# Probabilities as matmul weights for the retrieval heads of a sparse-attention and MoE kernel

## The chip, the cores and the metric

The kernel runs on one core of a Trainium2 chip. The metric is the device time of one execution in microseconds (us). The profile's span, from the first instruction to the last, is 1.7 us shorter than that time. Each group of kernels below was run on one chip together with runs of the kernel before. Undisturbed runs count as fast.

TensorE multiplies, VectorE (DVE) and ScalarE (ACT) do elementwise work, GpSimd (POOL) and SyncE (SP) issue DMAs. TensorE's results land in buffers of PSUM ("banks"; the tiles pA, pO and pV), and TensorE waits when the one that it needs has not been read out yet: 0.4 us for ScalarE's relu (hs) and 1.1 us for VectorE's accumulator (acc) in the profile before. "Evacuation" means this reading out.

## The reference

Eight attention heads over 4 batches of 768 positions, head width 64. Heads 0, 2 and 6 ("retrieval") see all earlier positions, the other five ("streaming") see 4 sink positions and a window of 64. Four experts follow, each two matrix products with a relu between, mixed by normalised domain probabilities.

```python
scores = scale * np.matmul(q, k.transpose(0, 1, 3, 2))
mask = np.where(retr, causal, causal & (is_sink | in_win))
a = np.exp(scores - max);  a = a / (a.sum(-1) + 1e-9)
x = np.matmul(a, v)                      # -> (3072, 512), heads side by side
p = domain_probs / (domain_probs.sum(-1) + 1e-9)
out = sum(p[:, e] * (np.maximum(x @ w1[e], 0) @ w2[e]) for e in range(4))
```

## The kernel before

The work goes in eight chunks of 384 positions, two for each batch. The MoE of chunk g runs on TensorE while the attention of chunk g+1 is mixed into it in small steps. The first chunk's attention stands alone, ahead of everything. The chunks of batch 0 transpose q and k on TensorE, the later ones by DMA. The value product of a head takes 128 columns of weights: 64 of values and 64 of ones, so that rows 64 to 127 of the result hold the sum of the probabilities, and the quotient is built as exp(-ln(sum)) on ScalarE and multiplied on VectorE, straight into xT, which the MoE reads with x's columns on partitions.

```python
def values(h):
    hp, u = divmod(h, 2)
    ps = pV.tile([P, 512], FP32, name="pV", bufs=2)
    # ... work: the head's pieces of probabilities
    for n, (es, t, o, q0, nq) in enumerate(work):
        nc.tensor.matmul(out=ps[:, q0 : q0 + nq], lhsT=v_tile(b, c, h)[:, t, :],
                         rhs=es[:, o : o + nq], start=(n == 0), stop=(n == len(work) - 1), ...)
    # ...
    nc.scalar.activation(out=rc[r, :], in_=ps[o, 0:CH], func=AF.Ln, bias=eps[o, :])
    def scale(r=r, ps=ps):
        nc.vector.tensor_tensor(out=xT[g][r, hp, :], in0=ps[r, 0:CH], in1=rc[r, :], op=ALU.mult)
    nc.scalar.activation(out=rc[r, :], in_=rc[r, :], func=AF.Exp, scale=-1.0)
    late.append(scale)          # issued after the next head's exponential
# ... later chunks:
    yield from scores(0)
    for h in range(1, H):
        if not by_dma and h % 2 == 0 and h // 2 + 1 < HP:
            yield from transposes(h // 2 + 1)      # two heads before they are read
        yield from both(scores(h), values(h - 1))
    yield from values(H - 1)
```

The softmax here doesn't subtract the row's maximum and nothing guards it: scores larger than these inputs give would overflow.

## Time and profile before

| | kernel before |
|---|---|
| time, first three runs | 413.33 us (413.29 to 413.35) |
| the two levels | 411.6 and 413.3 us; the profiled run took 411.59, the lower one |
| until the first MoE matmul | 22.87 us |
| first MoE chunk, with the second chunk's attention | 55.39 us |
| the rest | 331.64 us |

The three stretches are cut at the start of the first MoE matmul of chunk 0 and at that of chunk 1. This is the view of busy time in these three stretches; the columns are the stretch, its length, busy time with the number of instructions on TensorE, its weight loads, VectorE, ScalarE and GpSimd, then the granted TensorE clock (1.00 is full speed), the DMA share and GB/s. Lines of a timeline, further below and in the prediction, give the start and the length in us, the engine, the line of kernel.py, the operation, output<-input with shapes, and the count; in brackets how long the engine stood idle before and what released it.

```profile
0.00:22.87 22.87, 17.23 (x138) 12.49 (x139) 19.68 (x54) 13.46 (x28) 21.47 (x39) 1.00 1.25 163
22.87:78.26 55.39, 52.80 (x367) 29.64 (x365) 26.98 (x50) 34.86 (x77) 31.91 (x40) 1.00 1.49 183
78.26:409.90 331.64, 325.50 (x2169) 180.00 (x2167) 108.12 (x199) 192.56 (x404) 88.37 (x97) 1.00 0.72 81
```

In the last stretch TensorE has some 98% of the time; in the first, VectorE has 86% and TensorE less. The two need different reasoning. GpSimd's 21.47 us (94%) in the first stretch are for the most part the issuing of loads, about 13 us.

### The profile page before, as it was taken

The page shows a single profiled execution, that of the slowest core. Times are in us where ns is not written, and L with a number is a line of the kernel's source. Part 1 is how long each engine was busy: PE and PEld are TensorE (multiplying, and loading weights), DVE is VectorE, ACT ScalarE, POOL GpSimd, SP SyncE. Part 2 cuts the span into 40 slices and gives each one's busy share as a digit, 9 for nine tenths or more (in the row PEclk, how much of TensorE's full clock was granted, in tenths as well). Part 3 has the DMA queues.
Part 4 walks back from the last instruction along what each step waited for, and adds up shares of the span by engine and source line. Part 5 has one row for each costly group of instructions (what it writes and reads, how often), then busy time and mean ns, then how long its engine had stood idle before and what let it go on. Part 6 is the DMA issues. An engine that isn't in the chain of part 4 may idle for free.

```text
span 409.9 us, 6803 instructions
## 1 busy us (share of the span) xinstructions
PE 395.5 (97%) x2670; PEld 222.1 (54%) x2670; DVE 154.8 (38%) x302; ACT 240.9 (59%) x509; POOL 141.7 (35%) x176
## 2 busy tenths in 40 slices
PE   6789999999999999999999999999999999999995
PEld 4655555555555555555555555555555555545552
DVE  7975552224442234222423334224333233332222
ACT  2867874346775747566675548655665558653331
POOL 8946718459349268004920194000000000000000
PEclk9999999999999999999999999999999999999998
DMA  9999999999999999349964899149002000020002
GB/s 175 144 190 204 210 209 137 144 207 113 158 91 186 183 102 113 65 102 132 111 40 110 171 92 73 12 110 155 3 0 80 2 2 0 2 77 2 1 2 77
DMA packets 159988, 40.83 MB, mean 100 GB/s; under 512 B 150364, under 2 KB 154836, under 8 KB 159956
## 3 DMA queue, kind: packets, MB, share of 16 engines
q0 software_dynamic: 102592, 20.98, 61.0%
q1 hardware_dynamic: 54164, 18.62, 23.0%
q10 hardware_dynamic: 3200, 0.79, 1.0%
q8 instruction: 21, 0.34, 0.3%
q14 instruction: 11, 0.09, 0.1%
HBM read 43.57 MB, written 6.29 MB: 122 GB/s over the span
## 4 chain that ended last, share of the span: by engine, by line
PE 84%; ACT 9%; DVE 3%; issue 2%; DMA 1%; ACTq 0%; DVEq 0%
PE pO L749 38%; PE pA L728 36%; PE pA L561 4%; PE pV L609 4%; ACT rc L628 3%; ACT hs L741 2%; ACT rc L638 2%; ACT es L579 1%; DMA q<-in_q_dram 1%; DVE acc L765 1%; DVE vS L261 1%; DVE xT L633 1%; ACTq L328 0%; PE pO L355 0%; DVE kS L490 0%
## 5 line engine op out<-in xcount | busy, mean ns | idle before, releaser
L728 PE MATMUL pA<-xT,w1sb 128*128 128x384 f16 x1024 | 186.2, 326 | 2.1 <-DVE kS L490 0.9
L749 PE MATMUL pO<-w2sb,hs 128*128 128x512 f16 x768 | 180.5, 379 | 1.2 <-DVE acc L765 1.1
L741 ACT ACTIVATE hs<-pA 128x384 f16<-128x384 f32 x256 | 121.7, 493 | 86.3 <-PE pA L728 79.4
L728 PEld LDWEIGHTS <-w1sb 128*128 128x128 f16 x1024 | 96.5, 98 | 61.9 <-issue 2.7
L749 PEld LDWEIGHTS <-hs 128*128 128x128 f16 x768 | 72.9, 98 | 78.4 <-ACT hs L741 2.6
L765 DVE SCALAR_TENSOR_TENSOR acc<-pO,p_sb,acc 128x512 f32<-128x512 f32 x72 | 53.7, 750 | 86.8 <-PE pO L749 86.3
L579 ACT ACTIVATE es<-pA 128x512 f16<-128x512 f32 (+3 forms) x122 | 61.1, 512 | 21.0 <-PE pA L561 19.3
L628 ACT ACTIVATE rc<-pV,eps 64x384 f32<-64x384 f32 x60 | 34.5, 575 | 43.3 <-PE pV L609 42.3
L633 DVE TENSOR_TENSOR xT<-pV,rc 64x384 f16<-64x384 f32 x60 | 33.1, 552 | 26.2 <-ACT rc L638 22.5
L204 POOL DMA_DIRECT2D kSr<-in_k_dram x30 | 30.1, 1004 | 33.4 <-issue 13.1
L250 POOL DMA_DIRECT2D vS<-in_v_dram x30 | 30.4, 1025 | 26.1 <-PE pV L609 26.1
L200 POOL DMA_DIRECT2D kRr<-in_k_dram x18 | 14.1, 783 | 52.5 <-DMA kR<-kRr 48.5
L761 DVE TENSOR_SCALAR acc<-pO,p_sb 128x512 f32<-128x512 f32 x24 | 18.0, 750 | 37.4 <-PE pO L749 37.4
L638 ACT ACTIVATE rc<-rc 64x384 f32<-64x384 f32 x58 | 30.2, 521 | 1.8
L583 DVE TENSOR_TENSOR es<-es,mC 128x256 f16<-128x256 f16 (+1 forms) x42 | 10.8, 257 | 46.2 <-ACT es L579 45.9
L583 DVE TENSOR_TENSOR es<-es,mW 128x384 f16<-128x384 f16 x30 | 10.8, 359 | 44.6 <-ACT es L579 44.5
L561 PE MATMUL pA<-qT,kR 128*128 128x384 f16 (+2 forms) x120 | 25.0, 278 | 0.0
L609 PE MATMUL pV<-es,vR 128*128 128x384 f16 (+2 forms) x120 | 21.6, 278 | 0.0
L246 POOL DMA_DIRECT2D vR<-in_v_dram x24 | 19.2, 801 | 4.5 <-DMA w2sb<-in_moe_w_dram 4.4
L561 PEld LDWEIGHTS <-kS 128*128 128x128 f16 x255 | 13.7, 98 | 8.8 <-issue 2.0
L609 PEld LDWEIGHTS <-vS 128*128 128x128 f16 x255 | 13.4, 98 | 8.8 <-DVE vS L261 2.1
L561 PE MATMUL pA<-qT,kS 128*128 128x55 f16 (+4 forms) x255 | 16.4, 195 | 1.5 <-ACT es L579 1.4
(77 smaller groups left out, 159.0 us busy)
## 6 DMA issues: line engine op xcount, KB each, us to landing
out_dram<-acc SPq DMA_DIRECT2D x24, 256.0 KB
w1sb<-in_moe_w_dram POOLq DMA_DIRECT2D x4, 1024.0 KB, 15.2
w2sb<-in_moe_w_dram POOLq DMA_DIRECT2D x4, 1024.0 KB, 17.7
kSr<-in_k_dram POOLq DMA_DIRECT2D x30, 112.0 KB, 3.8
vS<-in_v_dram POOLq DMA_DIRECT2D x30, 112.0 KB, 4.4
q<-in_q_dram POOLq DMA_DIRECT2D x18, 128.0 KB, 4.3
vR<-in_v_dram POOLq DMA_DIRECT2D x24, 48.0 KB, 4.4
kRr<-in_k_dram POOLq DMA_DIRECT2D x18, 48.0 KB, 3.8
```

The lines of the kernel that those rows point to most:

```text
L204: gp.dma_start(out=kSr[:, :, SH.index(h), own(h)], in_=windows_of(k, b, h, c),)
L250: gp.dma_start(out=t[:, :, own(h)], in_=windows_of(v, b, h, c))
L561: nc.tensor.matmul(out=ps[:, o : o + nq], lhsT=key_tile(b, c, h, t), rhs=qTs[b, c][:, hp, q0 : q0 + nq], start=(n == 0 or not first), stop ...
L579: nc.scalar.activation(out=es[:, 0:cols], in_=ps[:, 0:cols], func=AF.Exp, scale=SC)
L609: nc.tensor.matmul(out=ps[:, q0 : q0 + nq], lhsT=v_tile(b, c, h)[:, t, :], rhs=es[:, o : o + nq], start=(n == 0), stop=(n == len(work) - 1 ...
L628: nc.scalar.activation(out=rc[r, :], in_=ps[o, 0:CH], func=AF.Ln, bias=eps[o, :])
L633: nc.vector.tensor_tensor(out=xT[g][r, hp, :], in0=ps[r, 0:CH], in1=rc[r, :], op=ALU.mult)
L638: nc.scalar.activation(out=rc[r, :], in_=rc[r, :], func=AF.Exp, scale=-1.0)
L728: nc.tensor.matmul(out=pss[ft][:, 0:CH], lhsT=w1sb[:, e * DMP + ct, ft * P : (ft + 1) * P], rhs=xT[g][:, ct, :], start=(ct == 0), stop=(ct ...
L741: nc.scalar.activation(out=hs[:, ft, :], in_=ps[:, 0:CH], func=AF.Relu)
L749: nc.tensor.matmul(out=ps_o, lhsT=hs[:, ft, j * P : (j + 1) * P], rhs=w2sb[:, e * FTP + ft, :], start=(ft == 0), stop=(ft == FTP - 1),)
L765: nc.vector.scalar_tensor_tensor(out=acc[nt], in0=ps_o, scalar=p_ap, in1=acc[nt], op0=ALU.mult, op1=ALU.add,)
```

## The change

Its intent: for retrieval heads, stop paying for 64 columns of ones. The probabilities become the weights, block by block, and 65 columns stream: 64 of values and one of ones. The result has queries on partitions, so the sum is one number for each partition, and the quotient needs no Ln and Exp. The price: x has to be transposed back, on TensorE in the first chunk and by DMA afterwards. To make pairs that fill a whole transpose, heads 2 and 6 share a column tile of xT, so head order changes to (h % 4, h // 4) in xT and in w1's rows. Heads of later chunks run in a new order, and the streaming heads' products are issued by a clock of matmul time, 1.3 us late.

```diff
-        vR.append(pers.tile([P, S // P, len(RH), P], FP16, name=f"vR{i}"))
+        vR.append(pers.tile([P, S // P, NR, D + 2], FP16, name=f"vR{i}"))
...
+        def values_r(h):
+            for n, (j, t, lhsT) in enumerate(work):      # 128x128 blocks of probabilities
+                nc.tensor.matmul(out=ps[:, j, 0 : D + 1], lhsT=lhsT,
+                                 rhs=vR[i][:, t, RH.index(h), 0 : D + 1], ...)
...
+            nc.vector.tensor_scalar(out=rs, in0=ps[:, :, D : D + 1], scalar1=1e-9, ..., op0=ALU.add)
+            nc.vector.reciprocal(out=rs, in_=rs)
+            nc.vector.tensor_tensor(out=x[:, :, half(u)], in0=ps[:, :, 0:D],
+                                    in1=rs.to_broadcast([P, 3, D]), op=ALU.mult)
+            if h != 2 and not first:
+                nc.sync.dma_start(out=xT[g][:, ct, :]..., in_=x..., transpose=True)
...
-            yield from scores(0)
-            for h in range(1, H):
-                if not by_dma and h % 2 == 0 and h // 2 + 1 < HP:
-                    yield from transposes(h // 2 + 1)
-                yield from both(scores(h), values(h - 1))
+            order = (0, 2, 6, 1, 3, 5, 7, 4) if by_dma else (0, 2, 1, 3, 6, 5, 7, 4)
+            for n, h in enumerate(order):
+                if not by_dma and n in (3, 5):
+                    yield from transposes(3 if n == 3 else 2)
+                yield from both(scores(h), iter(()) if last is None else values(last))
...
-                late.append(scale)
+                later(scale)                             # LAG = 1300.0 ns of matmul time
...
+                cts = (0, 1, 2, 3) if g == 0 else (2, 1, 3, 0)
```

Cut: the halves of w1's load, the fills of ones, the first chunk's calls of `x_transposes`.

More of the change, by code (lines that the diff above doesn't have):

```diff
@@ L62 @@
     RETR = (1, 0, 1, 0, 0, 0, 1, 0)
+    PLACE = [(h % HP, h // HP) for h in range(H)]
     RH = [h for h in range(H) if RETR[h]]
@@ L135, with half, own_v @@
     v_sinks = pers.tile([NS, 1, NSH * P], FP16, name="v_sinks")
+    x_pair = pers.tile([P, 3, P], FP16, name="x_pair")
+    x_one = pers.tile([P, 3, P], FP16, name="x_one")
+    def half(u):
+        return slice(u * D, (u + 1) * D)
     def own(h):
-        u = h % 2
-        return slice(u * D, (u + 1) * D)
+        return half(h % 2)
+    def own_v(h):
+        return half(PLACE[h][1])
     def key_tile(b, c, h, t):
@@ L246, in load_v @@
                 gp.dma_start(
-                    out=t[:, 3 * c : 3 * c + 3, own(h)], in_=rows_of(v, b, h, c)
+                    out=t[:, 3 * c : 3 * c + 3, 0:D], in_=rows_of(v, b, h, c)
                 )
@@ L250, in load_v @@
                 gp.dma_start(
-                    out=t[:, :, own(h)], in_=windows_of(v, b, h, c)
+                    out=t[:, :, own_v(h)], in_=windows_of(v, b, h, c)
                 )
@@ L254, in load_v @@
                 gp.dma_start(
-                    out=t[R0:P, TC * c : TC * (c + 1), own(h)],
+                    out=t[R0:P, TC * c : TC * (c + 1), own_v(h)],
                     in_=tiles_of(v, b, h, c),
@@ L259, in sink_row @@
     def sink_row(b, h, c):
-        t = v_tile(b, c, h)[:, :, own(h)]
+        t = v_tile(b, c, h)[:, :, own_v(h)]
         nc.vector.tensor_copy(
@@ L276, in load_w1 @@
     def load_w1(e, f0, f1):
-        gp.dma_start(
-            out=w1sb[:, e * DMP : (e + 1) * DMP, f0:f1],
-            in_=moe_w1[e].rearrange("(co ci) f -> ci co f", ci=P)[:, :, f0:f1],
-        )
+        x = moe_w1[e].rearrange("(u c d) f -> u d c f", u=2, c=DMP)
+        for u in range(2):
+            gp.dma_start(
+                out=w1sb[half(u), e * DMP : (e + 1) * DMP, f0:f1],
+                in_=x[u, :, :, f0:f1],
+            )
     def load_w2(e):
@@ L309, in one_values_r @@
         t = slice(3 * c, 3 * c + 3)
-        fill(eng, vR[i][:, t, :, D:P], ONES)
+        fill(eng, vR[i][:, t, :, D : D + 2], ONES)
     def one_values(eng, c):
@@ L316, in one_values @@
         fill(eng, vS[0:R0, t, :, :].rearrange("p t h x -> p t (h x)"), ONES)
-        fill(eng, vS[:, t, 0:2, 0:D], ONES)
-        fill(eng, vS[:, t, 2, D:P], ONES)
-        fill(eng, vS[:, t, 3:5, 0:D], ONES)
-    assert all(h % 2 == 0 for h in RH) and [h % 2 for h in SH] == [1, 1, 0, 1, 1]
+        fill(eng, vS[:, t, 0:2, D:P], ONES)
+        fill(eng, vS[:, t, 2:5, 0:D], ONES)
+    assert RH == [0, 2, 6] and [PLACE[h] for h in RH] == [(0, 0), (2, 0), (2, 1)]
+    assert [PLACE[h][1] for h in SH] == [0, 0, 1, 1, 1]
     q32 = moe.tile([P, 3, H, D], FP32, name="q32", tag="hs", bufs=2)
@@ L547, in attention @@
         scale_of = {}
-        late = []
-        def run_late():
-            while late:
-                late.pop(0)()
         def scores(h):
@@ L589, in scores @@
                 es_of[h].append((es, parts))
-                run_late()
+                if first:
+                    tick(LAG)
                 yield ns
+        def values_r(h):
+            ps = pV.tile([P, 512], FP32, name="pV", bufs=2)
+            if first:
+                warm_up(ps, {6: 8}.get(h, 0), 256)
+            ps = ps[:, 0 : 3 * (D + 2)].rearrange("p (j x) -> p j x", j=3)
+            work = []
+            for j in range(3):
+                for es, parts in es_of[h]:
+                    for t, o, q0, nq in parts:
+                        x = j * P - q0
+                        if 0 <= x < nq:
+                            work.append((j, t, es[:, o + x : o + x + P]))
+            ns = 0
+            for n, (j, t, lhsT) in enumerate(work):
+                nc.tensor.matmul(
+                    out=ps[:, j, 0 : D + 1],
+                    lhsT=lhsT,
+                    rhs=vR[i][:, t, RH.index(h), 0 : D + 1],
+                    start=(n == 0),
+                    stop=(n == len(work) - 1),
+                    skip_group_check=True,
+                )
+                ns += mm_ns(D + 1)
+                if ns > 200 and n < len(work) - 1:
+                    yield ns
+                    ns = 0
+            rs = att.tile([P, 3, 1], FP32, name="rs", bufs=2)
+            nc.vector.tensor_scalar(
+                out=rs, in0=ps[:, :, D : D + 1], scalar1=1e-9, scalar2=None,
+                op0=ALU.add,
+            )
+            nc.vector.reciprocal(out=rs, in_=rs)
+            ct, u = PLACE[h]
+            x = x_pair if ct else x_one
+            nc.vector.tensor_tensor(
+                out=x[:, :, half(u)], in0=ps[:, :, 0:D],
+                in1=rs.to_broadcast([P, 3, D]), op=ALU.mult,
+            )
+            yield ns
+            if h != 2 and not first:
+                nc.sync.dma_start(
+                    out=xT[g][:, ct, :].rearrange("p (j x) -> p j x", j=3),
+                    in_=x.rearrange("p j x -> p (j x)"),
+                    transpose=True,
+                )
@@ L593, in values, with x_transposes @@
+        def x_transposes(h):
+            ct = PLACE[h][0]
+            x = x_pair if ct else x_one
+            r = slice(0, P) if ct else half(0)
+            ps = pO.tile([P, 512], FP32, name="pO", bufs=2)
+            for j in range(3):
+                nc.tensor.matmul(
+                    out=ps[r, j * P : (j + 1) * P], lhsT=x[:, j, r], rhs=ident16,
+                    start=True, stop=True,
+                )
+            nc.vector.tensor_copy(out=xT[g][r, ct, :], in_=ps[r, 0:CH])
         def values(h):
-            hp, u = divmod(h, 2)
+            if RETR[h]:
+                yield from values_r(h)
+                return
+            ct, u = PLACE[h]
@@ L599, in values @@
             if first:
-                warm_up(ps, {3: 4, 4: 4, 5: 6, 6: 8, 7: 10}.get(h, 0), 256)
+                warm_up(ps, {3: 4, 4: 4, 5: 6, 7: 10}.get(h, 0), 256)
             work = []
@@ L604, in values @@
                     work.append((es, t, o, q0, nq))
-            if RETR[h]:
-                work.sort(key=lambda w: -w[4])
             ns = 0
@@ L620, in values @@
                     ns = 0
-            r = slice(u * D, (u + 1) * D)
-            o = slice((1 - u) * D, (2 - u) * D)
-            pair = first and hp < HP - 1
-            if u == 0 or not pair:
-                rc_of[hp] = att.tile([P, CH], FP32, name="rc", bufs=4)
-            rc = rc_of[hp]
+            r, o = half(u), half(1 - u)
+            pair = first and h in (3, 4)
+            if not pair or u == 0:
+                rc_of[0] = att.tile([P, CH], FP32, name="rc", bufs=4)
+            rc = rc_of[0]
             nc.scalar.activation(
@@ L633, in scale @@
                 nc.vector.tensor_tensor(
-                    out=xT[g][r, hp, :], in0=ps[r, 0:CH], in1=rc[r, :], op=ALU.mult
+                    out=xT[g][r, ct, :], in0=ps[r, 0:CH], in1=rc[r, :], op=ALU.mult
                 )
@@ L638, in values @@
                 nc.scalar.activation(out=rc[r, :], in_=rc[r, :], func=AF.Exp, scale=-1.0)
-                late.append(scale)
+                later(scale)
             elif u == 0:
-                scale_of[hp] = scale
+                scale_of[0] = scale
             else:
                 nc.scalar.activation(out=rc, in_=rc, func=AF.Exp, scale=-1.0)
-                late.extend([scale_of[hp], scale])
+                later(scale_of[0])
+                later(scale)
             yield ns
@@ L677, in attention @@
                 sinks(*{3: [4, 5], 5: [7]}.get(h, []))
+                if h == 3:
+                    x_transposes(0)
                 if h == 5:
@@ L681, in attention @@
             yield from values(H - 1)
+            x_transposes(H - 2)
         else:
             sink_rows(b, c)
-            yield from scores(0)
-            for h in range(1, H):
-                if not by_dma and h % 2 == 0 and h // 2 + 1 < HP:
-                    yield from transposes(h // 2 + 1)
-                yield from both(scores(h), values(h - 1))
-            yield from values(H - 1)
-        run_late()
+            order = (0, 2, 6, 1, 3, 5, 7, 4) if by_dma else (0, 2, 1, 3, 6, 5, 7, 4)
+            last = None
+            for n, h in enumerate(order):
+                if not by_dma and n in (3, 5):
+                    yield from transposes(3 if n == 3 else 2)
+                yield from both(scores(h), iter(()) if last is None else values(last))
+                last = h
+            yield from values(last)
     def small_things():
@@ L713, with later, tick @@
     sink_k = {}
+    behind = []
+    clock = [0.0]
+    LAG = 1300.0
+    def later(op):
+        behind.append((clock[0] + LAG, op))
+    def tick(ns):
+        clock[0] += ns
+        while behind and behind[0][0] <= clock[0]:
+            behind.pop(0)[1]()
     def moe_group(g):
@@ L725, in moe_group, with layer1 @@
                 pss = {ft: bank() for ft in range(f0, f0 + (1 if f0 else ahead))}
-                def layer1(ft, ct):
+                cts = (0, 1, 2, 3) if g == 0 else (2, 1, 3, 0)
+                def layer1(ft, n):
+                    ct = cts[n]
                     nc.tensor.matmul(
@@ L731, in layer1 @@
                         rhs=xT[g][:, ct, :],
-                        start=(ct == 0),
-                        stop=(ct == DMP - 1),
+                        start=(n == 0),
+                        stop=(n == DMP - 1),
                     )
@@ L771, in moe_group @@
                 yield FTP // 2 * mm_ns(DM)
+    nc.vector.memset(x_one[:, :, D:P], 0.0)
     warm_up(ps_warm, 8, 512)
-    for _ in attention(0, 0):
-        pass
+    for ns in attention(0, 0):
+        tick(ns)
+    tick(LAG)
     zero(gp, kRr)
@@ L798 @@
         end = {0: 2.2}.get(g, 0.90 * E) * UNIT
-        att_ns = 3700.0 if nxt % NCH == 0 else 6800.0
+        att_ns = 3500.0 if nxt % NCH == 0 else 5600.0
         if nxt < NCH:
@@ L807 @@
             spent += ns
+            tick(ns)
             if to_transpose and spent > 0.5 * E * UNIT:
@@ L815 @@
                 done += step
-        for _ in att_steps:
-            pass
+                tick(step)
+        for ns in att_steps:
+            tick(ns)
+        tick(LAG)
 _INS = ['q', 'k', 'v', 'is_retrieval', 'n_sink', 'window', 'moe_domain_probs', 'moe_w1', 'moe_w2']
```

## The prediction

> **What bounds the kernel now.** I read the page's busy table and clock row first, then its chain that ended last, then the groups by shape, and last the matmul stream itself in order of time.
>
> ```profile
> PE 395.5 (97%) x2670; PEld 222.1 (54%) x2670; DVE 154.8 (38%) x302; ACT 240.9 (59%) x509; POOL 141.7 (35%) x176
> PEclk9999999999999999999999999999999999999998
> PE 84%; ACT 9%; DVE 3%; issue 2%; DMA 1%; ACTq 0%; DVEq 0%
> ...
> L728 PE MATMUL pA<-xT,w1sb 128*128 128x384 f16 x1024 | 186.2, 326 | 2.1 <-DVE kS L490 0.9
> L749 PE MATMUL pO<-w2sb,hs 128*128 128x512 f16 x768 | 180.5, 379 | 1.2 <-DVE acc L765 1.1
> ...
> L628 ACT ACTIVATE rc<-pV,eps 64x384 f32<-64x384 f32 x60 | 34.5, 575 | 43.3 <-PE pV L609 42.3
> L633 DVE TENSOR_TENSOR xT<-pV,rc 64x384 f16<-64x384 f32 x60 | 33.1, 552 | 26.2 <-ACT rc L638 22.5
> ...
> L638 ACT ACTIVATE rc<-rc 64x384 f32<-64x384 f32 x58 | 30.2, 521 | 1.8
> ```
>
> The reader is to see three things: TensorE is busy 97% at full clock and holds 84% of the chain; the two MoE groups are most of it; and ScalarE and VectorE have room on average. But the "mean ns" of a matmul holds its latency; what a matmul costs a full stream is the distance from its start to the next start. Worked out from the trace's start times, the medians are 216 ns for 512 columns, 162 for 384, 109 for 256, 56 for 128, 42 for 96 and 28 for 54 to 64, all with a weight load in front of each. So the bill of the span of 409.9 us is: 22.9 us until the first MoE matmul; 1024 x 0.1625 + 768 x 0.216 = 332.3 us of MoE; about 43 us of attention matmuls of the later seven groups, mixed in; 4.0 us tail after the last matmul; and some 8 us left over, in which TensorE stands (about 3 before 60 us, 4.9 after). Any matmul nanosecond removed after 23 us comes off the time, one for one.
>
> **What the Trainium skill says.** "TensorE: Matmul & The Clock Gate", section Back-to-back issue gap, gives N/2.4 + 2.5 ns as the isolated gap and about 81 ns for 128 columns in a stream of weight load and matmul pairs. This trace agrees with the first (56 ns at 128, 42 at 96, 109 at 256, each with its own weights) and not with the second. The same page, LDWEIGHTS (loading the stationary operand), charges by weight columns, P/1.2 = 107 ns for 128; the rows here show 98 ns, yet pairs with 54 columns follow one another every 28 ns, so the loads overlap and don't set the pace above 28 ns. "ScalarE: Activation LUTs", section What ACT_TABLE_LOAD costs, gives 0.833 ns an element plus 186 ns, or 280 ns with a bias pointer: 506 and 600 ns for 384 elements; measured 521 and 575. "Perfetto Trace Analysis", section Optimizing Scalar/DVE Operations, puts VectorE's fixed cost from PSUM at about 125 ns; the 384-wide product took 552 = 400 (384 at 0.96 GHz) + 152, near that.
>
> **The change part by part.**
>
> Value matmuls of the three retrieval heads. Before, the values (padded to 128 columns by ones) were the weights and 128 to 384 probabilities streamed. The groups by shape count 48 of 384 columns, 36 of 256, 36 of 128: 48 x 0.1625 + 36 x 0.109 + 36 x 0.056 = 13.7 us (13.8 by the starts). A first-half chunk's head is seen whole here, 93.06 to 93.39 = 0.33 us for three matmuls, and a stream of short pairs beside it: seven in 0.36 us, of which 0.19 is the last one's latency, so 28 ns apart:
>
> ```profile
> 93.06 0.49 PE L609 MATMUL pV<-es,vR 128*128 128x384 f16 x3
> 93.39 1.46 PE L728 MATMUL pA<-xT,w1sb 128*128 128x384 f16 x8
> ...
> 137.44 0.36 PE L609 MATMUL pV<-es,vS 128*128 128x54 f16 x7
> ```
>
> After, each 128x128 block of probabilities is a weight and 65 columns stream. Blocks are columns / 128: 6 in a first-half chunk, 15 in a second-half chunk, so 21 x 3 heads x 4 batches = 252 matmuls. At 65/2.4 + 2.5 = 29.6 ns (between the 28 measured at 64 and 42 at 96) that is 7.5 us. Saved 6.3 us, of which 0.45 lies in the very first chunk, where TensorE isn't the bound: **-5.8 us** on the path.
>
> The quotient. Before, ScalarE did Ln (575) and Exp (521) per head and VectorE the product (552). After, retrieval heads use VectorE alone: an add on 3 elements, a reciprocal on 3 (a 24-element pair of these took 178 + 302 ns; I take 300 for both), and a 192-wide product, 200 + 152 = 350: 0.65 us. VectorE gains 24 x 0.1 = 2.4 us, unnoticed at 38%. ScalarE loses 24 x 1.1 = 26 us, idle time nobody waits for, except where its bursts stop TensorE. The matmul stream shows the same five stops in each pair of groups, three times over: 0.31 us at 139.6 and 0.15 at 187.7 (Ln and Exp sit before the relu or the exponential that must free a PSUM bank), 0.30 at 152.6, 0.21 at 156.6, and the longest here:
>
> ```profile
> 169.76 0.52 ACT L638 ACTIVATE rc<-rc 64x384 f32<-64x384 f32 x1
> 170.31 0.56 DVE L633 TENSOR_TENSOR xT<-pV,rc 64x384 f16<-64x384 f32 x1 [1.11 <-ACT rc L638]
> 170.91 1.41 DVE L765 SCALAR_TENSOR_TENSOR acc<-pO,p_sb,acc 128x512 f32<-128x512 f32 x2
> 171.68 0.99 SPq L770 DMA_DIRECT2D out_dram<-acc  x2
> 171.71 1.02 PE L749 MATMUL pO<-w2sb,hs 128*128 128x512 f16 x4 [0.37 <-DVE acc L765]
> ```
>
> Here VectorE, in order, waits 1.11 us for ScalarE's Exp while a finished accumulator waits behind it, and TensorE stops for the bank (0.53 us by the starts). Retrieval heads now come first, so no Ln and Exp mixes with the 512-wide exponentials, and the products of the other heads are issued 1.3 us of matmul time later. I expect four of the five stops to go and 0.30 to stay: **-3.5 us** of the 4.9.
>
> Transposes. Queries now lie on partitions, so two DMA transposes of 128x384 per later group carry x back to xT, on SyncE. The three transposes of q (128x512 each) take 4.1 to 4.9 us of the queue a group, so about 1.2 us each here. Pair and single are done by some 60% of the previous group at the latest, over 15 us before they are read: hidden, **0**.
>
> The first chunk. It transposes on TensorE (6 matmuls, 0.3 us) with two more VectorE copies of 0.55 us each. VectorE is the bound there: 9.35 of the 10 us from 10 to 20. From 10 us on to the first MoE matmul it did 7 products (3.9 us); now 4 products (2.2), 3 quotients (2.0), 2 copies (1.1): +1.4 us. ScalarE loses 2.2 us in the same stretch, which pays part back, and the last pieces (head 6's transposed copy, head 5's product) come just as MoE starts, where the kernel before had no wait: **+0.9 us**.
>
> w1 is loaded in halves: one more issue of 0.75 us on GpSimd for each expert, with the DMA engines full. The first w1 landed at 20.9 us and was read at 22.9, the second at 37.9 and was read at 39.9: 2 us of room: **0**. The fills of ones shrink: 0.2 us on VectorE before its data arrives: **0**.
>
> Sum: -5.8 - 3.5 + 0.9 = -8.4 us; 413.3 - 8.4 = 404.9.
>
> **Rivals.** (1) The small matmuls run slower than 29.6 ns, because every one has fresh weights that ScalarE and VectorE have just written. For it: none of the present streams loads weights from es. Against: streams of 54 columns with their own weights keep 28 ns. At 42 ns the saving falls by 3.1 us: 408. (2) The start eats more: x_transposes and the deferred products chain TensorE, VectorE, TensorE and VectorE just before MoE, and +2.5 us instead of 0.9 gives 406.5. (3) SyncE becomes the bound: a transpose of x waits for VectorE, and the next transposes of q and k wait behind it in the queue. For it: the queue is in order and its k transposes last 5 to 9 us. Against: those start over 20 us before use. If it struck, a microsecond or more per group: 410 or worse. (4) All stops go, also the 3 us before 60 us: 401.
>
> **Range and chances.** The matmul saving I hold to within 1 us, the stops within 1.5 and the start within 1. Rivals 1 and 2 pull up, 4 pulls down. Centre 404.7, range 401.5 to 408.5. The line of 2% is 405.1, almost at the centre; so 0.53 faster, 0.46 the same, 0.01 slower.
>
> **What would show it.** Value matmuls from vR: 252 of 65 columns, starts 29 to 31 ns apart. ScalarE busy near 215 us, VectorE near 158. Stops of TensorE after 60 us down from 4.9 to about 1.5 us, none behind the accumulators. First MoE matmul near 23 us with a stop of about a microsecond in the first dozen. Transposes of x landing 10 us or more before the group that reads them. The prediction is wrong if the matmuls are spaced 40 ns, if new waits on VectorE or DMA appear at group starts, or if the first chunk grows by over 2 us.

## The result, and the profile after

| | before | after |
|---|---|---|
| median of the runs of the comparison | 413.31 us (411.56 to 413.35) | 407.66 us (407.65 to 409.28) |
| lower level, upper level | 411.6, 413.3 | 407.65, 409.28 |
| until the first MoE matmul | 22.87 | 25.22 |
| first MoE chunk with the second chunk's attention | 55.39 | 58.12 |
| the rest | 331.64 | 322.56 |

The ratio is 0.9883 (95% interval 0.9848 to 0.9919): the same at the 2% mark. Ratios are the mean time of one kernel's fast runs over that of the other's of the same rounds, so not quite the ratio of the medians in the table. Most of the kernels have two levels about 1.7 us apart. The medians differ by 5.65 us, but before's is of its upper level and after's of its lower one; level against level the change is worth 4.0 us at both (411.6 to 407.65, and 413.3 to 409.28). The lower levels are the safer pair, since the upper ones need not have one cause (see a_lead).

The page of the kernel after, in its parts that answer to those shown of before:

```profile
PE 390.8 (96%) x2808; PEld 221.5 (55%) x2808; DVE 159.2 (39%) x352; ACT 218.4 (54%) x463; POOL 142.2 (35%) x179
PEclk9899999999999999999999999999999999999999
PE 89%; DVE 5%; ACT 2%; issue 1%; POOL 1%; POOLq 0%; DVEq 0%; ACTq 0%
...
L700 ACT ACTIVATE rc<-pV,eps 64x384 f32<-64x384 f32 x37 | 21.3, 575 | 13.0 <-PE pV L682 12.5
```

ScalarE's share of the chain has gone from 9% to 2%, VectorE's from 3% to 5%: the bound is purer TensorE, with a new piece of VectorE. Its busy time of Ln, Exp and the rest fell by 22.5 us. The same three stretches:

```profile
0.00:25.22 25.22, 19.49 (x154) 14.22 (x154) 20.38 (x62) 11.60 (x24) 21.68 (x40) 0.93 1.26 158
25.22:83.34 58.12, 52.54 (x391) 29.18 (x389) 27.65 (x55) 32.39 (x71) 32.47 (x42) 1.00 1.54 181
83.34:405.90 322.56, 318.82 (x2268) 178.12 (x2266) 111.16 (x235) 174.36 (x368) 88.10 (x97) 1.00 0.73 86
```

The reader is to see where the time went: -9.08 us in the long last stretch, +2.35 and +2.73 us in the two short ones in front of it. In the second stretch TensorE is even busy for 0.3 us less than before and yet the stretch is longer: it stands. The value matmuls of one head of a first-half chunk, which took 0.33 us before, in order of time:

```profile
107.59 0.34 PE L621 MATMUL pV<-vR,es 128*128 128x65 f16 x6
107.78 1.46 PE L822 MATMUL pA<-xT,w1sb 128*128 128x384 f16 x8
```

From 107.59 to the next matmul at 107.78 is 0.19 us for six. By the trace's starts their median distance is 29 ns, over all 252. And where TensorE waits, longest first (engine and line, for whom, us in total, times, longest):

```profile
PE pV L682 <- DVE es L595: 2.1, 2, 1.4
PE pA L573 <- DVE qT L483: 1.9, 1, 1.9
PE pA L573 <- ACT es L591: 1.8, 2, 1.0
```

Counting every distance between starts that is over 40 ns longer than columns / 2.4 + 2.5 ns, at least 28 ("stops" from here on), the last stretch has 0.3 us of stops where before had 4.3. The second stretch has 8.4 where before had 4.6. The longest stop of all, 2.1 us by the starts, at 53.0 us:

```profile
52.02 1.61 DVE L508 CAST kS<-pA 64x384 f16<-64x384 f32 x2
...
52.88 0.36 PE L475 MATMUL pA<-ident,q 128*64 128x128 f16 x6
53.66 0.75 DVE L859 SCALAR_TENSOR_TENSOR acc<-pO,p_sb,acc 128x512 f32<-128x512 f32 x1
54.33 0.79 DVE L483 CAST qT<-pA 128x384 f16<-128x384 f32 x1
55.17 0.34 PE L573 MATMUL pA<-qT,kS 128*128 128x64 f16 x3 [1.94 <-DVE qT L483]
```

TensorE has transposed q of heads 4 and 5 at 52.9 us, and its next instruction, the scores of head 5, needs the copy of that transpose. VectorE still has two key copies and an accumulator ahead of it. The new order calls `transposes(2)` right before `scores(5)`; the old one called each two heads earlier.

### The profile page after: what moved, and what is told of

Read it like the earlier page. It is cut to its first block, busy times and chain, and to the rows that moved or that the text cites. A ratio compares the mean times of both kernels' runs of the same rounds, so it can differ in the third digit from the quotient of the medians.

```text
span 405.9 us, 7079 instructions
## 1 busy us (share of the span) xinstructions
PE 390.8 (96%) x2808; PEld 221.5 (55%) x2808; DVE 159.2 (39%) x352; ACT 218.4 (54%) x463; POOL 142.2 (35%) x179
## 4 chain that ended last, share of the span: by engine, by line
PE 89%; DVE 5%; ACT 2%; issue 1%; POOL 1%; POOLq 0%; DVEq 0%; ACTq 0%
PE pO L843 40%; PE pA L822 39%; PE pA L573 5%; PE pV L621 2%; PE pV L682 2%; DVE kS L508 1%; ACT es L591 1%; ACT hs L835 1%; DVE vS L277 1%; ACT rc L700 1%; DVE kR L492 1%; PE pA L472 1%; DVE vS L321 0%; DVE xT L705 0%; DVE qT L483 0%
## 5 line engine op out<-in xcount | busy, mean ns | idle before, releaser
L843 PEld LDWEIGHTS <-hs 128*128 128x128 f16 x768 | 71.7, 98 | 73.2 <-ACT hs L835 0.7
L591 ACT ACTIVATE es<-pA 128x384 f16<-128x384 f32 (+2 forms) x122 | 61.1, 509 | 58.6 <-PE pA L573 54.8
L705 DVE TENSOR_TENSOR xT<-pV,rc 64x384 f16<-64x384 f32 x37 | 20.5, 553 | 27.6 <-ACT rc L710 21.6
L595 DVE TENSOR_TENSOR es<-es,mC 128x256 f16<-128x256 f16 (+1 forms) x42 | 10.8, 259 | 49.5 <-ACT es L591 48.6
L700 ACT ACTIVATE rc<-pV,eps 64x384 f32<-64x384 f32 x37 | 21.3, 575 | 13.0 <-PE pV L682 12.5
L710 ACT ACTIVATE rc<-rc 64x384 f32<-64x384 f32 x38 | 19.8, 521 | 1.2
L595 DVE TENSOR_TENSOR es<-es,mW 128x384 f16<-128x384 f16 x30 | 10.7, 357 | 17.1 <-ACT es L591 17.1
L621 PEld LDWEIGHTS <-es 128*128 128x128 f16 x252 | 13.4, 98 | 7.2 <-issue 0.2
```

Source lines behind the costliest of these rows:

```text
L591: nc.scalar.activation(out=es[:, 0:cols], in_=ps[:, 0:cols], func=AF.Exp, scale=SC)
L595: nc.vector.tensor_tensor(out=es[:, o0:o1], in0=es[:, o0:o1], in1=m[:, mo : mo + o1 - o0], op=ALU.mult,)
L621: nc.tensor.matmul(out=ps[:, j, 0 : D + 1], lhsT=lhsT, rhs=vR[i][:, t, RH.index(h), 0 : D + 1], start=(n == 0), stop=(n == len(work) - 1), ...
L843: nc.tensor.matmul(out=ps_o, lhsT=hs[:, ft, j * P : (j + 1) * P], rhs=w2sb[:, e * FTP + ft, :], start=(ft == 0), stop=(ft == FTP - 1),)
```

## The experiments

The theory after this reading (A): the steady part gained what the matmuls and the missing ScalarE work promise, and the first 83 us gave more than half of it back through VectorE's order of work. The rivals are named with each run. In the diffs, lines of the changed kernel are marked minus unless said otherwise.

| run | time (all runs, us) | first MoE matmul | first MoE chunk | rest |
|---|---|---|---|---|
| before | 411.6 or 413.3 | 22.87 | 55.39 | 331.64 |
| after | 407.65, 407.66, 407.66, 409.28 | 25.22 | 58.12 | 322.56 |
| a_lead | 406.1, 406.02, 406.02, 406.07 | 25.26 | 56.48 | 322.6 |
| a_small | 406.95, 408.68, 408.77, 407.05 | 24.40 | 58.11 | 322.6 |
| a_fill | 411.1, 409.33, 409.61, 409.61 | 27.00 | 59.79 | 322.6 |
| a_double | 415.06, 413.35, 415.01, 413.35 | 25.22 | 59.79 | 328.29 |
| b_sched | 413.86, 411.82, 411.79, 413.51 | 24.31 | 56.05 | 331.74 |
| a_lag0 | 410.96, 412.53, 410.96, 414.25 | 25.25 | 60.43 | 323.52 |
| a_natural | 409.58, 409.55, 407.9, 409.54 | 25.26 | 59.75 | 322.89 |
| best1 | 407.41, 408.47, 407.37, 414.19 (slow) | 25.96 | 56.90 | 322.8 |
| a_act | 421.32, 421.05, 421.23, 421.35 | 25.25 | 62.69 | 331.66 |
| b_noact | 408.11, 409.87, 409.86, 409.83 | 22.89 | 54.75 | 328.76 |
| best2 | 415.88, 414.15, 415.23, 417.31 | 24.43 | 64.43 | 325.3 |
| best3 | 405.31, 405.33, 406.31, 405.3 | 24.40 | 56.49 | 322.61 |

The first time of each row but the first two is of the profiled run, to which the stretches belong. In every run but b_noact the result was correct.

### What a value matmul costs: a_double

```diff
                 nc.tensor.matmul(out=ps[:, j, 0 : D + 1], lhsT=lhsT, rhs=..., start=(n == 0), ...)
+                if b:
+                    nc.tensor.matmul(out=ps[:, j, 0 : D + 1], lhsT=lhsT, rhs=..., start=False, ...)
```

> The changed kernel with every 65-column value matmul of batches 1 to 3 issued twice (values and row sums both double, so the quotient is right). 21 blocks x 3 heads x 3 batches = 189 more matmuls. Theory A (TensorE bounds the steady part and such a matmul costs 29 to 30 ns): time rises by 5.4 to 5.7 us to about 413.2 us. Rival B (weight loads of freshly written probabilities cost about 40 ns each): plus 7.6 us. Rival C (part of these matmuls fills idle time): under plus 4 us.

The last stretch, in which all 189 lie, grew from 322.56 to 328.29 us: 5.73 / 189 = 30.3 ns each, with stops unchanged at 0.3 us.

```profile
85.01:413.30 328.29, 324.52 (x2457) 183.86 (x2455) 111.26 (x235) 174.52 (x368) 88.09 (x97) 1.00 0.76 86
```

The times rose by 5.7 us as well, level by level (407.65 to 413.35). So the steady part is bound by TensorE's stream. Weights that ScalarE and VectorE have just written cost no more than others: the first of each pair is the one that reads them fresh, and these are 29 ns apart in the changed kernel. Theory A holds; both rivals fall.

### The second chunk's transposes: a_lead

```diff
-                if not by_dma and n in (3, 5):
-                    yield from transposes(3 if n == 3 else 2)
+                if not by_dma and n in (1, 3):
+                    yield from transposes(3 if n == 1 else 2)
```

> The changed kernel with one edit: in the second chunk's attention the TensorE transposes of the last two head pairs are issued two head steps earlier (before the second and fourth head instead of the fourth and sixth). Theory A (the lost gain lies in the second chunk, where the transposes of heads 4 and 5 are now issued right before the scores that read them): the 2.1 us stop of TensorE at 53 us goes, time 405.5 to 406.2 us. Rival B (only the first chunk lost time, the rest of the second chunk is bound by the arriving weights): no change, 407.7 us.

Measured 406.0 us in all four runs. The first MoE chunk fell from 58.12 to 56.48 us, and the stop at 53 us is gone: TensorE now goes on with 512-wide MoE matmuls at the same place.

```profile
53.59 0.33 PE L573 MATMUL pA<-qT,kS 128*128 128x64 f16 x3
53.76 1.03 PE L843 MATMUL pO<-w2sb,hs 128*128 128x512 f16 x4
```

The run did a second thing that was not expected: no run of it shows the upper level. What that level is can be seen in a_natural's trace, which has the changed kernel's second chunk with the stop still in it. These are windows of busy time, first of the changed kernel, then of a_natural: the stop, and what follows it. The third number from the right is the granted clock.

```profile
53.00:55.20 2.20, 0.27 (x7) 0.11 (x6) 2.08 (x3) 0.00 (x0) 0.00 (x0) 1.00 1.18 212
55.45:58.86 3.41, 3.41 (x37) 2.00 (x35) 1.84 (x6) 1.36 (x3) 1.93 (x2) 1.00 1.13 209
```

```profile
53.00:55.20 2.20, 0.27 (x6) 0.11 (x7) 2.11 (x3) 0.00 (x0) 0.42 (x1) 1.00 1.23 209
55.99:59.40 3.41, 3.41 (x25) 1.96 (x24) 1.03 (x3) 0.46 (x2) 0.97 (x1) 0.50 1.12 209
```

In a_natural the stop is followed by 3.41 us at half clock, which costs half of it, 1.7 us: the distance of the two levels. In the changed kernel's profile the same stop passed unpunished. The Trainium skill, "TensorE: Matmul & The Clock Gate", Part 1: The HAM clock gate, has a free-running activity window of 3413 ns, and an array that was idle through one falls to half clock; the 3.41 us and the 0.50 here agree, and a window that isn't tied to the program explains that the same stop is caught in one run and not in the next.

The other traces bear this out. a_double, a_fill and a_act have the same stop of 2.1 us, and behind it 3.41 us at half clock, from 55.45, 57.11 and 56.83 us on; the first two were profiled in runs of the upper level. In all four traces with the spell the whole stop lies within the 3.41 us before it. In the three with the stop and without the spell (the changed kernel, a_small, a_lag0) an edge falls inside the stop, at 53.96, 53.46 and 56.24 us, when one counts in steps of 3.413 us from a change of the clock in the same trace (at 13.00, 5.67 and 5.04 us).

That the unprofiled upper runs had such a window too is inferred from the same 1.7 us, not seen. For the kernel before no upper run has a trace. The profiled run of b_sched, which shares its first chunk, is an upper one (413.86 us) and has its half clock elsewhere: from 7.84 to 14.66 us, with the first MoE matmul at 24.31 us instead of 22.87.

The changed kernel's profile has such a window in its first chunk, from 9.59 to 13.00 us (the 8 in its clock row), and that one costs nothing: a_natural had full clock there and began its MoE at 25.26 us instead of 25.22. At that place the first chunk is not bound by TensorE.

### VectorE in the first chunk: a_small

```diff
                 sinks(*{3: [4, 5], 5: [7]}.get(h, []))
-                if h == 5:
-                    small_things()
...
             yield from transposes(1)
+            if not first:
+                small_things()
```

> The changed kernel with the ten small VectorE instructions (masks, normalised domain probabilities, 2 us together) moved from the first chunk behind the second chunk's first transposes. Theory A (VectorE bounds the first chunk): the first MoE matmul comes near 23.5 us instead of 25.2, time about 406.2 us. Rival B (the first chunk lost time by the half clock from 9.6 to 13.0 us and the late mask of GpSimd, which stand before these instructions): no change, 407.7 us.

The first MoE matmul came at 24.40 us, 0.8 us earlier, and the lower level fell by 0.7 us to 406.95: neither the 1.7 us of A nor the nothing of B. VectorE does bound the end of the first chunk, but once its 2 us are gone others take over within 0.8: it waits for ScalarE's Exp, TensorE for head 6's quotient.

```profile
22.81 0.56 DVE L705 TENSOR_TENSOR xT<-pO,rc 64x384 f16<-64x384 f32 x1 [0.61 <-ACT rc L710]
...
23.81 0.36 DVE L641 TENSOR_TENSOR x_pair<-pV,rs 128x192 f16<-128x192 f32 x1
24.60 0.56 DVE L663 CAST xT<-pO 128x384 f16<-128x384 f32 x1 [0.44 <-PE pO L659]
```

This is the price of the new form at that place: the quotient (three instructions), a transpose on TensorE, a copy, and only then the column tile that the third MoE matmul reads. The upper level stays in two of the four runs, as the stop at 53 us does.

### GpSimd's wait at the start: a_fill

```diff
-        fill(eng, vS[:, t, 2:5, 0:D], ONES)
+        for n in (2, 3, 4):
+            fill(eng, vS[:, t, n, 0:D], ONES)
```

> The changed kernel with the fill of ones of three neighbouring heads issued as three fills, as the kernel before had it in pieces. Theory A (VectorE bounds the first chunk from 13 us on): GpSimd's second load no longer waits 1.26 us for VectorE, the mask bS is ready before it is needed and the stop of 0.6 us at 9.2 us goes, but the first MoE matmul moves by under 0.8 us; time 407.0 to 407.7 us. Rival B (this wait delays the whole first chunk): the first MoE matmul comes near 23.5 us and the time is about 406 us.

The wait went: the second load was issued at 2.40 us instead of 3.67. But the kernel became 1.7 us slower at the lower level, and neither theory had said so. The first MoE matmul came at 27.00 us, after two windows of half clock (9.33 to 12.74 and 19.57 to 22.98), the second behind a stop of 1.8 us at 17.1 us for VectorE. VectorE was held there by one copy of 4x256 elements that took 2.12 us; the shortest of these copies takes 0.22, and 12 of the 14 traces, before and after among them, have one of over 2 us in the first chunk. Why was not tested. This second window:

```profile
19.57:22.98 3.41, 3.41 (x24) 2.80 (x23) 3.06 (x15) 2.04 (x4) 3.41 (x6) 0.50 1.61 196
```

So the start of the program is not made faster by removing one wait; what arrives earlier meets other work elsewhere. Why all four runs were 1.7 us or more slower is open: only one has a trace, and that one, at 411.1 us, also holds the half clock behind the stop of the second chunk.

### What took the stops of the steady part away: b_sched, b_noact, a_lag0, a_natural, a_act

The kernel before with the new schedule alone:

```diff
-                late.append(scale)
+                (late.append if first else later)(scale)
...
+            order = (0, 2, 6, 1, 3, 5, 7, 4) if by_dma else tuple(range(H))
```

(with `later` and `tick` taken over from the changed kernel)

> The kernel before, value matmuls and Ln and Exp as they were, with only the new schedule: in batches 1 to 3 the retrieval heads first (0, 2, 6, 1, 3, 5, 7, 4), and the products of all later chunks issued 1.3 us of matmul time later. Theory A (the stops of TensorE after 60 us were made by the order and by products queued too early, not by the amount of ScalarE work): most of the 4.9 us of stops go, time 408.5 to 410 us against 413.3. Rival B (the 23 us less of ScalarE work in the later chunks took the stops away): under 1.5 us faster, 412 us or more.

The last stretch took 331.74 us against 331.64, with 4.4 us of stops against 4.3: the schedule alone gives nothing in sum. It did change which stops there are: the one behind the accumulators shrank from 0.53 to 0.17 us, three times, and new ones of 0.65 and 0.62 us, three times each, took the place of the others. The TensorE waits of b_sched name ScalarE's relu for 3.2 us of the time.

```profile
PE pA L742 <- ACT hs L755: 3.2, 7, 0.5
```

The kernel before with only the ScalarE work removed:

```diff
+            skip = RETR[h] and not first        # rc = a constant tile, no Ln, no Exp
+            if skip: late.append(scale)         # result wrong on purpose
```

> The kernel before with Ln and Exp of the retrieval heads left out in the later chunks (their product takes a constant instead; the result is wrong on purpose), nothing else changed. Theory A (ScalarE's work made the stops): the stretch after the second chunk falls from 331.6 to 327.5 to 329 us, time 2.5 to 4 us under the kernel before. Rival B (order or delay needed): under 1 us.

331.64 fell to 328.76 us, stops from 4.3 to 1.5, and each level by 3.5 us. So 21 pairs of Ln and Exp less on ScalarE are worth 2.9 us by themselves, in the old order and with the old delay. The run takes away two things at once, though: this work, and VectorE's wait for its result. The stop behind the accumulators, which hung on that wait, fell from 0.53 to 0.08 us, three times; those of 0.30 and 0.21 us, three times each, went altogether. Which part of the 2.9 us belongs to the work and which to the wait is not separated. ScalarE was busy for 192.56 of 331.64 us in the kernel before, 58%: its average load doesn't explain the stops, the place of its bursts does.

The changed kernel without the delay, and with the natural order in batches 1 to 3:

```diff
-    LAG = 1300.0
+    LAG = 0.0
```

> The changed kernel with the delay of the products set from 1.3 us to nothing (they are issued at the next step). Theory A (the delay is what removed the stop behind the accumulators, 0.53 us three times): plus 1 to 2 us, 408.7 to 409.7 us. Rival B (with less ScalarE work it is not needed): no change, 407.7 us, or faster in the first two chunks.

```diff
-            order = (0, 2, 6, 1, 3, 5, 7, 4) if by_dma else (0, 2, 1, 3, 6, 5, 7, 4)
+            order = tuple(range(H)) if by_dma else (0, 2, 1, 3, 6, 5, 7, 4)
```

> The changed kernel with the heads of batches 1 to 3 in their natural order 0 to 7 instead of the retrieval heads first. Theory A (the order keeps Ln and Exp away from the 512-wide exponentials, 0.8 us of stops in each of three pairs of chunks): plus 1.5 to 2.5 us. Rival B (with 3 of 8 Ln and Exp pairs gone the order is free): within 0.5 us of 407.7 us.

Without the delay the last stretch grows by 0.96 us (323.52) and the first MoE chunk by 2.3 us, where there is no spell of half clock in the trace; 3.3 us in all, more than expected, and most of it in the second chunk. The natural order costs 0.33 us (322.89): nearly free, as rival B had it. Its three runs at 409.5 are the upper level explained above. So 2.9 + 0.96 + 0.33 = 4.2 us stand against the 4.0 us of stops that went: the ScalarE work with VectorE's wait for it is most of it, the delay about a quarter, the order next to nothing. These are no exact shares: the 2.9 are measured in the old schedule, the other two in the new one, and the same delay and order gave nothing in the kernel before.

The reverse, the removed ScalarE work put back without use:

```diff
+            if not first:
+                again = att.tile([P, 2, 3, D], FP32, name="again", bufs=2)
+                nc.scalar.activation(out=again[half(0)], in_=ps[half(0), :, 0:D]..., func=AF.Exp, ...)
+                nc.scalar.activation(out=again[half(0)], in_=again[half(0)], func=AF.Exp, scale=-1.0)
```

> The changed kernel with the removed ScalarE work put back without any use: in the later chunks, two Exp instructions of 64x384 follow each retrieval head's value matmuls (21 heads x 1.1 us), reading its PSUM tile and writing a tile that nobody reads; the result stays right. Theory A (the amount of ScalarE work made the stops of TensorE after 60 us): with heads and delay of the new schedule, stops after the second chunk go from 0.3 to 2 us or more, so plus 2 to 4 us, 409.5 to 411.5 us. Rival B (VectorE's dependence on ScalarE made them, or the order): stops stay under 1 us, under 408.7 us.

421.2 us: theory A's direction, but twice its size and more. The last stretch took 331.66 us, 9.1 more, with 9.4 us of stops. One of them:

```profile
160.46 0.58 ACT L647 ACTIVATE again<-pV,eps 64x384 f32<-64x384 f32 x1 [0.40 <-PE pA L832]
...
161.06 0.52 ACT L652 ACTIVATE again<-again 64x384 f32<-64x384 f32 x1
...
161.49 0.47 ACT L591 ACTIVATE es<-pA 128x384 f16<-128x384 f32 x1
161.87 0.84 ACT L845 ACTIVATE hs<-pA 128x384 f16<-128x384 f32 x2
162.01 0.97 PE L832 MATMUL pA<-xT,w1sb 128*128 128x384 f16 x5 [0.80 <-ACT es L591]
```

1.1 us of ScalarE work, queued between two evacuations of PSUM banks, makes TensorE stand for 0.96 us by the starts. The run shows that such work is not free at 54% load. It isn't the exact reverse of the change: the added instructions keep the head's PSUM tile in use for longer, and in the new schedule these instructions fall on other places than in the old one, so its 9.1 us say nothing of before's 4.3.

### Put together: best1, best2, best3

best1 has the edits of a_lead, a_small and a_fill.

> The changed kernel with all three edits: transposes of the second chunk two steps earlier, small VectorE instructions after the first chunk, fill of ones in single heads. Theory A (the first two chunks lost some 5 us by VectorE's order of work): 403.5 to 404.7 us. Rival B (the stops only move, since VectorE's work in the first 70 us is the same): 406 us or more.

407.4 us at its lower level: worse than a_lead alone. Its trace has the first MoE matmul at 25.96 us, behind 6.83 us of half clock from 9.21 us: a_fill's loss came along. Against best3, which lacks the fills alone, its lower level is 2.1 us higher. The run of 414.19 us is slow and is left out.

best2 leaves a_fill away and spreads the second chunk's attention:

```diff
-        end = {0: 2.2}.get(g, 0.90 * E) * UNIT
+        end = {0: 3.0}.get(g, 0.90 * E) * UNIT
```

> The changed kernel with the transposes of the second chunk two steps earlier, the small VectorE instructions after the first chunk, and the second chunk's attention spread to 3.0 expert units instead of 2.2. Theory A (stops in the second chunk, 6.7 us with the earlier transposes alone, come from attention packed too densely for ScalarE and VectorE): 402.5 to 404.5 us. Rival B (the spread moves the stops or delays the next chunk): 405.3 us or more, which is what the first two edits alone should give.

415 us, a stop of 10.8 us at 77.9. SyncE's queue, in order of time, first of best2, then of a_lead with the old spread:

```profile
71.88 3.83 SPq L246 DMA_TRANSPOSE qT<-q  x3
...
77.80 8.05 SPq L252 DMA_TRANSPOSE kS<-kSr  x1
85.95 1.21 SPq L647 DMA_TRANSPOSE xT<-x_pair  x1
```

```profile
57.46 1.18 SPq L647 DMA_TRANSPOSE xT<-x_pair  x1
...
72.02 3.83 SPq L246 DMA_TRANSPOSE qT<-q  x3
```

With the later spread the transpose of x_pair stands in the program behind the next chunk's transposes of q and k, which wait for loads until 70 us and take 14 us of the queue. It was issued at 85.95 us, and the MoE of chunk 1 waited for it. This is the third rival of the prediction, the in-order queue of SyncE. The theory behind the run was not refuted by it: without the 10.8 us the stops of this stretch sum to 4.0 us, where best3 has 6.7, and those of 1.5 and 0.9 us behind VectorE's masks are gone. The changed kernel steers clear of it, by the 2.2 of its spread.

best3 is a_lead and a_small alone.

> The changed kernel with two edits only: the second chunk's transposes two steps earlier and the small VectorE instructions after the first chunk; fills and spread as in the changed kernel. Theory A (the two gains add up: 1.6 us in the second chunk, 0.7 us in the first): 405.0 to 405.6 us, all runs within 0.3 us since the 2.1 us stop is gone. Rival B (the moved VectorE instructions come back as a wait in the second chunk): 406 us or more, or two levels 1.7 us apart.

405.3 us in three runs, 406.31 in one (its ratio to before 0.9836, interval 0.9802 to 0.9870): the two gains add up, and it beats both kernels. By the 2% mark it is still the same. The odd run has no trace; its 1.0 us is unexplained.

## Why the prediction was right or wrong

The measured 407.66 us lies in the range, 3 us above the centre, and the verdict is "same", which had 0.46. That the number fits is in part luck: the sum was taken off 413.3, the upper level, while the trace it was read from is of a run of the lower one (411.59). Taken off 411.6, the same -8.4 gives 403.2, and the same range would have ended at 406.8, below the 407.65 of the changed kernel's lower level. One of the prediction's own signs of being wrong also came true: the first chunk grew by over 2 us (2.35). Point by point:

- **Value matmuls: right.** 29.6 ns each was forecast; the starts are 29 ns apart, and the doubled ones cost 30.3. Rival 1 (42 ns) is out.
- **TensorE time off the path, one for one: right** in the last stretch, where the forecast share of the 5.8 us is 4.7 (9 heads of 0.37 and 9 of 0.15) and the stops' 3.5. Together 8.2; measured 9.08. The stops fell by 4.0, more than forecast: the one of 0.30 us, which was to stay, went too. The reason given was half right: b_noact shows ScalarE's work and VectorE's wait for it as the main cause, not the order of heads that the prediction named first; the delay was worth about a quarter. (The stops before 60 us, "about 3" in the prediction, are 4.0 us by the counting used here.)
- **ScalarE and VectorE busy times: nearly right** (218.4 and 159.2 us for "near 215" and "near 158"; ScalarE lost 22.5 us of the 26 forecast), and so is the quotient, 0.16 + 0.18 + 0.36 = 0.70 us for 0.65. The 400 ns that the prediction puts down to 384 elements agree with the trace: VectorE's casts from PSUM take 0.16 us for 4 elements a partition and 0.56 for 384.
- **DMA transposes hidden: right** in the changed kernel (1.2 us of the queue each; a pair's transpose was issued at 252.60, the chunk that reads it begins at 268.1). best2 shows how near rival 3 was.
- **"The first chunk ... +0.9": mis-sized.** The term measured +2.35. Rival 2 had put it at 2.5. The term counted VectorE's work, and mainly its waits grew: from 10 us to the first MoE matmul VectorE was busy for 12.86 us where before had 12.06, and idle for 2.36 where before had 0.81. The longest wait, for TensorE's transposes of k, is 2.19 us at 11.4 us; before it was 0.92 at 10.2. Taking VectorE's ten small instructions out gives 0.8 us back (a_small); that they cost so much in the kernel before too is not excluded, since they stood in its first chunk as well. The other 1.5 us were not taken apart: quotient and transpose of head 6 stand in front of the first MoE matmul, as rival 2 said, while the copy after them makes TensorE stop for 0.5 us only behind it, in the second stretch. The fills of ones, forecast at 0, brought GpSimd a new wait of 1.26 us, whose cost a_fill could not show. (The prediction's seven products of the kernel before are six by the trace: the seventh starts 0.08 us after the first MoE matmul.)
- **The second chunk: the step that is missing.** The sum gave it -1.1 us, its share of the matmuls, and rival 4 allowed only that its stops would go. It measured +2.73. "Retrieval heads now come first" was weighed for the chunks of batches 1 to 3 alone; that the second chunk's new order puts `transposes(2)` directly before its reader stood in the diff and was not followed through. a_lead gives 1.64 of the 3.8 us; the stops that remain there (1.5 us at the last head's probabilities, 1.0 and 0.9 at key copies and masks on VectorE) are not settled: best2 thinned them out from 6.7 to 4.0 us in all, but ran into SyncE's queue, so what this is worth in time was not measured.
- **The sum.** At equal levels -8.4 was forecast and -4.0 measured, which is further off than the medians make it look: the errors are +1.45, +3.8 and -0.9, together +4.4.

## What to carry to other kernels

A change that reorders work has to be walked through for every phase that has its own schedule, the start above all: this one gained 9.1 us in four fifths of the time and gave 5.1 back in the rest, where the longest stops that were traced had TensorE waiting for VectorE. An engine at 58% can stop the one at 98%: ask what its bursts hold up, not what its average is. And when a kernel's times come in two levels, find which of them the trace belongs to before taking sums off the other.

## What the Trainium skill lacked or had wrong

- "TensorE: Matmul & The Clock Gate", Back-to-back issue gap: the 81 ns for 128 columns in a stream of loads and matmuls doesn't hold here. Medians by start are 56 ns at 128 columns and 29 at 65, each with its own weights; doubled 65-column matmuls cost 30.3 ns each. The section's other formula, N/2.4 + 2.5, fits all of them down to 65.
- The same page, Part 1: The HAM clock gate, has the clock fall after an idle window of about 3.4 us. Here a stop of 2.1 us, with 0.27 us of matmuls in 2.2, was followed by 3.41 us at half clock in four traces and by none in three others, with runs 1.7 us apart. A shorter stop was enough here where it lay whole within the 3.41 us before the spell, and not where an edge cut it (the figures are given with a_lead).
- "VectorE: DVE Perf Modes", The three transpose paths, has a DMA transpose of 128x128 only, with 1309 ns. For 128x384 between places of SBUF, two bytes an element, SyncE's queue was held for 1.18 and 1.21 us in the lines above, and the traces don't show when the data landed.
- No page says what happens when DMA transposes that wait for different producers share one issuing queue. Here the order in that queue cost a stop of 10.8 us (best2).
